# Attention followed by routed experts on one Trainium2 core: raw weight pieces loaded two ahead, gate product two units behind its rows' copy, decoding steps spread anew

## The chip, the cores and the metric

The kernel runs on one core of a Trainium2 chip. The metric is the device time of one execution in microseconds (us); the figure for the kernel before is the median of three runs. Engines: PE is TensorE (matmuls and transposes), DVE is VectorE, ACT is ScalarE, POOL is GpSimd, and SP issues most of the DMAs. Each engine works its own queue of instructions in order.

## What is computed

Three stages, each fed by the one before:

```python
# attention: 4 batches, 8 heads, 768 positions, 64 wide; a local band of 96 and 8 global keys
scores = scale * (q @ k.T) - slope[h] * dist;  a = softmax(where(keep, scores, -1e9));  x = a @ v
# experts: 3072 tokens, each expert takes at most 384, greedily by the highest logit
logits = x @ w_gate
for e in range(8): out[mask_e] = relu(x[mask_e] @ w1[e]) @ w2[e]
# gated network, weights w1, w2, w3, w_out held in float64
y = ((out @ w1) * (out @ w2)) @ w3 @ w_out
```

## The kernel before

**Attention.** The work is 96 items: for each of 16 pairs (a batch b and two heads) three steps p, each with two query tiles, and per step the two heads. A loop over units i (line 383) interleaves them: at every even i it multiplies queries and keys for both heads of a step (`scores`, L313) and reduces them on DVE (L318, bias, scaling and row minimum in one instruction), with the exponential on ACT (L329). Three units later `flip` transposes the probabilities on PE (L342; copied out by ACT, L349), and two more units later `values` multiplies them with v (L362). At a head's last step DVE divides (L368 to L370) into a tile x. A pair is thus six units long.

**Rows and gate.** When both heads of a pair are divided, `rows` (lines 410 to 420) is put into a list `after` for a later unit, twice per pair for three tiles each (z = 0 and 1). It stores x to DRAM, transposes it on PE into a PSUM tile px (L419), and ACT copies that to xt (L420). `gate` (lines 422 to 432) multiplies xt with the gate weights on PE into the last quarter of the same px tile (L427), and DVE adds the result to the logits L (L432; L430 for the first pair of a batch). The pool of px has one buffer: the next `rows` may write it only once L432 has read it. `self.line` keeps PE's attention work in the order in which it is written.

**Decoding.** The last network's weights lie in DRAM as float64 and are decoded to float32 beside attention, 40 pieces of 128x512. `stream` does it in steps: a load into a raw tile (L805, on SP), ACT takes the absolute value of the high words (`size`, L813), POOL clamps it (L837), and DVE puts the bits together (L843, L844, L846). Then ACT and POOL split a piece in two (L202, L207), or a DMA from POOL writes it to DRAM (L851). The function `beside` draws steps from this generator, or from the router's bids while there are any, at slots of each unit: z = 1 before `flip`, z = 2 behind `values`; the table SLOTS says how many. In the program a piece has three steps. Pools: `stage` two raw buffers, `vs` two, `ms` one.

**After attention.** The router searches the first expert's tokens (DVE and PE in turn) while PE folds w3 and w_out together (`fold`); then eight experts run, each with its weights loaded and split, and with the gated network behind it. The plain copies of w1 and w2 are loaded through the same `stream` and `stage` (L802).

**Order.** A scheduler places the instructions on the queues; the lists above fix PE's attention order, and marks keep decoding from moving ahead of attention on DVE and ACT.

Of the kernel before, what the change touches and what calls it, by code (L numbers as in the profile page):

```python
# [147 lines left out]
LAG3 = 2  # L148
# [3 lines left out]
class Net:  # L152
# [84 lines left out]
    def attention(self, ctx, beside, done):  # L237
# [11 lines left out]
        xs = self.pool(ctx, "xs", 2)  # L249
# [3 lines left out]
        ps_x = self.pool(ctx, "ps_x", 1, True)  # L253
# [28 lines left out]
        work = [(b, 2 * g + z, p) for b, g in pairs for p in range(half) for z in range(2)]  # L282
        qk, vs, pr_, pt_, po_, xs_ = {}, {}, {}, {}, {}, {}
# [47 lines left out]
        def flip(b, h, p):  # L331
            pr = pr_.pop((b, h, p))
            todo = [(i, c) for i in range(2) for c in range(len(plan.chunks[2 * p + i]))]
            size = lambda z: plan.chunks[2 * p + z[0]][z[1]][1]
            at = pt_[b, h, p] = {}
            for o in range(0, len(todo), 4):
                grp = todo[o:o + 4]
                pt = ps_t.tile([P, 512], F32, name="one").rearrange("p (c n) -> p c n", n=P)
                ptb = wk.tile([P, 4, P], F32, name=f"ptb{o}")
                for z, (i, c) in enumerate(grp):  # L340
                    c0, m = plan.chunks[2 * p + i][c]
                    self.line(nc.tensor.transpose(pt[:m, z], pr[:, i, c0:c0 + m], self.ident))  # L342
                    at[i, c] = ptb[:m, z]
                z = 0
                while z < len(grp):
                    m, y = size(grp[z]), z + 1
                    while y < len(grp) and size(grp[y]) == m:
                        y += 1
                    nc.scalar.activation(ptb[:m, z:y], pt[:m, z:y], AF.Copy)  # L349
                    z = y  # L350
# [21 lines left out]
        def ahead(f, u):  # L372
            if u < len(pairs):
                f(*pairs[u])

        lag1, lag2 = LAGS
        after = {}
# [2 lines left out]
            for t in range(min(T, 2)):  # L380
                head_bias(t, 0, 0, 1)
        ahead(load, 1)
        for i in range(len(work) + lag2 + 8):
            if i < len(work):
                if i % T == 0:
                    ahead(load_v, i // T)
                    ahead(load, i // T + 2)
                beside(i, 0)
                if i % 2 == 0:
                    scores(work[i][0], work[i][1] // 2, work[i][2])  # L390
            beside(i, 1)
            if 0 <= i - lag1 < len(work):
                flip(*work[i - lag1])
            if 0 <= i - lag2 < len(work):
                w = work[i - lag2]
                values(*w)
                if w[1] % 2 and w[2] == half - 1:
                    b, g = w[0], w[1] // 2
                    x = xs_.pop((b, g))
                    for z in range(2):  # L400
                        after.setdefault(i + LAG3 + 2 * z, []).append((self.rows, (b, g, 3 * z, x, xs, ps_x)))
                        after.setdefault(i + LAG3 + 2 * z + 1, []).append((self.gate, (b, g, 3 * z)))
                    if g == G - 1:
                        after[i + LAG3 + 3].append((done, (b,)))
            beside(i, 2)
            for f, args in after.pop(i, []):
                f(*args)
# [366 lines left out]
class Experts:  # L774
# [41 lines left out]
    def stream(self, todo):  # L816

        nc, V = self.nc, self.nc.vector
        dve = lambda ins: self.net.aside(ins, "dve")
        raw = self.load(*todo[0][:2])
        yield
        m = self.size(raw, todo[0][1])
        yield
        for i, (_, n, v, parts, dst) in enumerate(todo):
            after = self.load(*todo[i + 1][:2]) if i + 1 < len(todo) else None  # L830
            if m is None:
                if v is None:
                    v = raw
                else:
                    nc.scalar.activation(v, raw, AF.Copy)
            else:
                nc.gpsimd.tensor_scalar(m, m, MOST, LEAST, op0=OP.min, op1=OP.max)  # L837
                yield
                if v is None:
                    v = self.vs.tile([P, 512], F32, name="v")[:, :n]  # L840
                pair = raw.bitcast(I32).rearrange("p (n t) -> p n t", t=2)
                lo, hi, mi, vi = pair[:, :, 0], pair[:, :, 1], m.bitcast(I32), v.bitcast(I32)
                dve(V.tensor_scalar(vi, mi, 3, 0x3FFFFFFF, op0=OP.logical_shift_left, op1=OP.bitwise_and))  # L843
                dve(V.scalar_tensor_tensor(vi, hi, -0x40000000, vi, op0=OP.bitwise_and, op1=OP.bitwise_or))  # L844
                yield
                dve(V.scalar_tensor_tensor(vi, lo, 29, vi, op0=OP.logical_shift_right, op1=OP.bitwise_or))  # L846
            if parts is not None:
                parts = parts() if callable(parts) else parts
                self.net.split(*parts, v, nc.scalar, self.low())
            if dst is not None:  # L850
                nc.gpsimd.dma_start(dst, v)  # L851
            if after is not None:
                m, raw = self.size(after, todo[i + 1][1]), after
            yield

    def decode(self):
# [183 lines left out]
PRIME = 28  # L1040
GAP = 1
SOON = 1
SLOTS = (0, 1, 1), (0, 1, 0), (0, 1, 1)
PIN = 3
BEGIN = 7
START = 98
# [6 lines left out]
def steps(gen, n):  # L1053
    for _ in range(n):
        if next(gen, STOP) is STOP:
            return
# [5 lines left out]
def network(ctx, tc, plan, a, out):  # L1062
    net = Net(ctx, tc, plan, a, out)
    ex = Experts(net)
# [1 line left out]
    ex.res2 = net.pool(ctx, "res2", ex.JT // 2)  # L1066
    keep = net.pool(ctx, "keep0")
    ex.ring = net.pool(ctx, "ring", RING)
    ex.stage = net.pool(ctx, "stage", 2)
    ex.vs = net.pool(ctx, "vs", 2)  # L1070
    ex.ms = net.pool(ctx, "ms")
    one = net.pool(ctx, "pone", 1, True)
    net.one = one
    bank = lambda: one.tile([P, 512], F32, name="one")
# [2 lines left out]
    ro = Router(net, ctx)  # L1077
    ro.ps = one
    with ExitStack() as inner:
        decode = ex.decode()  # L1080
        folds = (s for i in range(SOON) for s in ex.fold(i, keep, ex.ring, bank))
        bids = []

        def beside(i, z):
            if i == SETUP and z == 1:
                ro.setup()
            if i >= BEGIN:
                for _ in range(SLOTS[i % 3][z]):
                    if bids and next(bids[0], STOP) is STOP:
                        bids.pop(0)  # L1090
                    elif not bids:
                        steps(decode, 1)
            if i >= START and z == 1:
                steps(folds, RATE)

        net.attention(inner, beside, lambda b: bids.append(ro.bids(slice(b * net.T, (b + 1) * net.T), True)))
        for g in (decode, folds, *bids[:-1]):
            for _ in g:
                pass
        steps(bids[-1], 3)  # L1100
# [15 lines left out]
    inner = ex.rest = ex.inner()  # L1116
# [15 lines left out]
    for i in range(net.E):  # L1132
# [4 lines left out]
        done, soon = False, HEAD  # L1137
        for s, _ in enumerate(ex.run(now, route is None)):
# [8 lines left out]
            elif not done:  # L1147
                if s >= PRIME:
                    done = next(prime, STOP) is STOP
# [29 lines left out]
```

## Time and profile before

| what | before |
|---|---|
| median of 3 runs (range) | 1060.22 us (1055.45 to 1064.94) |
| the profiled execution: time / span | 1060.28 / 1058.5 us |
| PE busy | 1018.3 us (96%) |
| DVE, ACT, POOL busy | 652.7, 397.4, 125.8 us |
| mean granted TensorE clock | 0.963 |
| attention, about 5 to 257 us | PE busy, clock 0.86 |
| experts, 325 us on | PE busy, clock 1.00 |

Times are from one profiled execution; a busy time counts an engine's instructions from start to modelled end. [...] A wait is idle time of an engine just before an instruction, with what ended it.

### The profile page before, as it was taken

The numbers are of one execution on the slowest core, as the hardware profiler recorded it, in microseconds if no ns is written. First come the engines' busy times: TensorE is split into PE (matmuls) and PEld (weight loads), VectorE is DVE, ScalarE is ACT, GpSimd is POOL, SyncE is SP. The second block draws the span as 40 slices with busy tenths as digits, with TensorE's granted clock in tenths as the row PEclk, the third lists the DMA queues.
The fourth block names the chain that finished last, engine by engine and source line by source line (L and its number), as shares of the span: only waits on it lengthen the run. The fifth ranks groups of instructions, "written<-read, shape, count | busy, mean of one in ns | idle before, by whom it ended". The sixth has DMA issues, their size and how long they took to land.

```text
span 1058.5 us, 17537 instructions
## 1 busy us (share of the span) xinstructions
PE 1018.3 (96%) x6348; PEld 931.8 (88%) x6348; DVE 652.7 (62%) x2136; ACT 397.4 (38%) x841; POOL 125.8 (12%) x171
## 2 busy tenths in 40 slices
PE   7999998999989999999999999999999999999996
PEld 6888887888768889999998899999889999999995
DVE  5678676584789773856767485586747556423311
ACT  4677666575225422322422332242133224313311
POOL 1331111223350002001100200110020012001001
PEclk9799788698999999999999999999999999999999
DMA  5677767673015312203200320320132033302100
GB/s 219 193 223 242 246 182 253 217 235 129 16 50 169 110 60 70 91 1 108 91 22 30 112 79 1 110 100 11 41 110 70 2 110 115 105 1 75 35 1 30
DMA packets 53862, 107.57 MB, mean 102 GB/s; under 512 B 5648, under 2 KB 17936, under 8 KB 53776
## 3 DMA queue, kind: packets, MB, share of 16 engines
q1 hardware_dynamic: 48512, 89.65, 26.5%
q0 software_dynamic: 5120, 16.78, 4.6%
q8 instruction: 50, 0.82, 0.3%
q14 instruction: 36, 0.29, 0.1%
q10 hardware_dynamic: 144, 0.02, 0.0%
HBM read 89.65 MB, written 16.78 MB: 101 GB/s over the span
## 4 chain that ended last, share of the span: by engine, by line
PE 72%; issue 9%; DVE 8%; DMA 6%; ACT 4%; POOL 1%; POOLq 0%; SPq 0%; ACTq 0%; DVEq 0%
PE wk L789 11%; PE wk L790 10%; PE wk L791 10%; PE one L789 8%; PE one L791 8%; PE one L790 8%; PE po L362 5%; DMA raw<-in_m_dram 4%; PE one L313 3%; PE one L342 3%; PE one L530 2%; PE px L427 2%; DMA raw<-m_plain 2%; ACT p L329 1%; DVE A L446 1%
## 5 line engine op out<-in xcount | busy, mean ns | idle before, releaser
L789 PE MATMUL wk<-y,res 128*128 128x384 f32 x512 | 176.8, 346 | 0.1
L791 PE MATMUL wk<-y,res 128*128 128x384 f32 x512 | 172.8, 338 | 0.0
L790 PE MATMUL wk<-y,res 128*128 128x384 f32 x512 | 172.4, 337 | 0.1
L1013 DVE TENSOR_TENSOR g<-g,wk 128x384 f32<-128x384 f32 x64 | 35.4, 554 | 129.9 <-PE wk L791 125.2
L202 ACT ACTIVATE w<-wraw 128x512 fp32r<-128x512 f32 x128 | 80.0, 629 | 80.1 <-DMA wraw<-in_w_dram 39.1
L362 PE MATMUL po<-v,ptb 116*128 116x65 f32 (+1 forms) x704 | 105.9, 299 | 2.2 <-PE one L342 2.1
L362 PEld LDWEIGHTS po<-v,ptb 116*128 116x128 f32 (+1 forms) x704 | 103.7, 224 | 4.1 <-PE one L342 3.7
L329 ACT ACTIVATE p<-s,mx 128x232 f32<-128x232 f32 (+1 forms) x192 | 81.9, 466 | 53.6 <-DVE mx L318 53.3
L207 DVE TENSOR_TENSOR w<-wraw,w 128x512 fp32r<-128x512 f32 x128 | 86.2, 687 | 19.5 <-ACT w L202 18.3
L790 PEld LDWEIGHTS wk<-y,res 128*128 128x128 f32 x512 | 96.2, 188 | 2.1 <-DVE y L997 0.4
L789 PEld LDWEIGHTS wk<-y,res 128*128 128x128 f32 x512 | 96.1, 188 | 2.0 <-ACT y L996 0.3
L791 PEld LDWEIGHTS wk<-y,res 128*128 128x128 f32 x512 | 96.1, 188 | 0.0
L1012 ACT ACTIVATE g<-wk 128x384 f32<-128x384 f32 x64 | 31.4, 491 | 152.2 <-PE wk L791 130.1
L789 PE MATMUL wk<-x,w 128*128 128x384 f32 x256 | 87.9, 343 | 0.0
L789 PE MATMUL one<-h,w 128*128 128x384 f32 x256 | 87.0, 340 | 0.0
L791 PE MATMUL one<-h,w 128*128 128x384 f32 x256 | 86.8, 339 | 0.0
L790 PE MATMUL wk<-x,w 128*128 128x384 f32 x256 | 86.6, 338 | 0.1
L790 PE MATMUL one<-h,w 128*128 128x384 f32 x256 | 86.3, 337 | 0.0
L791 PE MATMUL wk<-x,w 128*128 128x384 f32 x256 | 86.1, 336 | 0.0
L318 DVE CUSTOM_DVE_ANT_0 s<-one,bias 128x232 f32<-128x232 f32 (+1 forms) x192 | 66.3, 374 | 30.5 <-PE one L313 30.2
L922 POOL DMA_INDIRECT xg<-x_rows,idx x24 | 25.4, 1057 | 482.8 <-issue 398.5
L1015 ACT ACTIVATE h<-g 128x384 fp32r<-128x384 f32 x64 | 33.4, 522 | 120.7 <-DVE g L1013 120.7
(186 smaller groups left out, 2033.5 us busy)
## 6 DMA issues: line engine op xcount, KB each, us to landing
wraw<-in_w_dram SPq DMA_DIRECT2D x128, 256.0 KB, 2.8
raw<-in_m_dram SPq DMA_DIRECT2D x32, 512.0 KB, 4.6
v<-in_v_dram SPq DMA_DIRECT2D x32, 357.5 KB, 3.4
k<-in_k_dram SPq DMA_DIRECT2D x16, 404.0 KB, 6.0
q<-in_q_dram SPq DMA_DIRECT2D x16, 384.0 KB, 3.9
x_rows<-x SPq DMA_DIRECT2D x32, 192.0 KB, 5.4
raw<-in_mo_dram SPq DMA_DIRECT2D x8, 512.0 KB, 4.8
m_plain<-v POOLq DMA_DIRECT2D x16, 256.0 KB, 4.6
```

Source lines behind the costliest of these rows:

```text
L202: self.aside(he.activation(hi, raw, AF.Copy), "act")
L207: self.aside(le.tensor_tensor(lo[:, c], raw[:, c], hi[:, c].bitcast(F32), op=OP.subtract), "dve" if le is self.nc.vector else "pool")
L313: self.line(nc.tensor.matmul(banks[y][:, 256 * z:256 * z + m], q[r, qt], k[r, kt], start=True, stop=True))
L318: self.mark["dve"] = nc.vector.tensor_tensor_reduce(out=s[y][:, i, c0:c0 + m], in0=banks[y][:, 256 * z:256 * z + m], in1=head_bias(2 * p + ...
L329: self.mark["act"] = nc.scalar.activation(pr[:, i, :n], s[y][:, i, :n], AF.Exp, bias=m1, scale=-1.0)
L342: self.line(nc.tensor.transpose(pt[:m, z], pr[:, i, c0:c0 + m], self.ident))
L362: self.line(nc.tensor.matmul(po[:, t], at[i, c], v[:m, plan.nch[t] + c], start=c == 0, stop=c == last))
L789: mm(out, w[0], x[0], start=start, stop=False)
L790: mm(out, w[0], x[1], start=False, stop=False)
L791: self.net.beat = mm(out, w[1], x[0], start=False, stop=stop)
L1013: V.tensor_tensor(g, g, two[1], op=OP.mult)
L1015: nc.scalar.activation(h[:, 0], g, AF.Copy)
```

## The change

In `stream` two raw pieces are under way ahead of the one being decoded, instead of one, and `stage` has three buffers. In `attention` the second `rows` of a pair comes three units behind the first instead of two, and each `gate` two units behind its `rows` instead of one; the loop is a unit longer. SLOTS is now a table over six units instead of three: as many steps per six units (ten), with one step behind `values` in the units where a head is divided (i mod 6 is 3 and 4) and none before `flip`. The pools `vs` and `ms` move into the attention's own scope. In the changed file lines behind 825 stand one further down (L843, L844, L846 are L844, L845, L847).

```diff
@@ -380,7 +380,7 @@
             for t in range(min(T, 2)):
                 head_bias(t, 0, 0, 1)
         ahead(load, 1)
-        for i in range(len(work) + lag2 + 8):
+        for i in range(len(work) + lag2 + 9):
             if i < len(work):
                 if i % T == 0:
                     ahead(load_v, i // T)
@@ -398,10 +398,10 @@
                     b, g = w[0], w[1] // 2
                     x = xs_.pop((b, g))
                     for z in range(2):
-                        after.setdefault(i + LAG3 + 2 * z, []).append((self.rows, (b, g, 3 * z, x, xs, ps_x)))
-                        after.setdefault(i + LAG3 + 2 * z + 1, []).append((self.gate, (b, g, 3 * z)))
+                        after.setdefault(i + LAG3 + 3 * z, []).append((self.rows, (b, g, 3 * z, x, xs, ps_x)))
+                        after.setdefault(i + LAG3 + 3 * z + 2, []).append((self.gate, (b, g, 3 * z)))
                     if g == G - 1:
-                        after[i + LAG3 + 3].append((done, (b,)))
+                        after[i + LAG3 + 5].append((done, (b,)))
             beside(i, 2)
             for f, args in after.pop(i, []):
                 f(*args)
@@ -822,12 +822,13 @@
 
         nc, V = self.nc, self.nc.vector
         dve = lambda ins: self.net.aside(ins, "dve")
-        raw = self.load(*todo[0][:2])
+        raws = [self.load(*z[:2]) for z in todo[:2]]
         yield
-        m = self.size(raw, todo[0][1])
+        m = self.size(raws[0], todo[0][1])
         yield
         for i, (_, n, v, parts, dst) in enumerate(todo):
-            after = self.load(*todo[i + 1][:2]) if i + 1 < len(todo) else None
+            raw = raws.pop(0)
+            raws += [self.load(*z[:2]) for z in todo[i + 2:i + 3]]
             if m is None:
                 if v is None:
                     v = raw
@@ -849,8 +850,8 @@
                 self.net.split(*parts, v, nc.scalar, self.low())
             if dst is not None:
                 nc.gpsimd.dma_start(dst, v)
-            if after is not None:
-                m, raw = self.size(after, todo[i + 1][1]), after
+            if raws:
+                m = self.size(raws[0], todo[i + 1][1])
             yield
 
     def decode(self):
@@ -1040,7 +1041,7 @@
 PRIME = 28
 GAP = 1
 SOON = 1
-SLOTS = (0, 1, 1), (0, 1, 0), (0, 1, 1)
+SLOTS = ((0, 1, 1),) * 3 + ((0, 0, 1),) * 2 + ((0, 1, 1),)
 PIN = 3
 BEGIN = 7
 START = 98
@@ -1066,9 +1067,7 @@
     ex.res2 = net.pool(ctx, "res2", ex.JT // 2)
     keep = net.pool(ctx, "keep0")
     ex.ring = net.pool(ctx, "ring", RING)
-    ex.stage = net.pool(ctx, "stage", 2)
-    ex.vs = net.pool(ctx, "vs", 2)
-    ex.ms = net.pool(ctx, "ms")
+    ex.stage = net.pool(ctx, "stage", 3)
     one = net.pool(ctx, "pone", 1, True)
     net.one = one
     bank = lambda: one.tile([P, 512], F32, name="one")
@@ -1077,6 +1076,8 @@
     ro = Router(net, ctx)
     ro.ps = one
     with ExitStack() as inner:
+        ex.vs = net.pool(inner, "vs", 2)
+        ex.ms = net.pool(inner, "ms")
         decode = ex.decode()
         folds = (s for i in range(SOON) for s in ex.fold(i, keep, ex.ring, bank))
         bids = []
@@ -1085,7 +1086,7 @@
             if i == SETUP and z == 1:
                 ro.setup()
             if i >= BEGIN:
-                for _ in range(SLOTS[i % 3][z]):
+                for _ in range(SLOTS[i % 6][z]):
                     if bids and next(bids[0], STOP) is STOP:
                         bids.pop(0)
                     elif not bids:
```

PE, a pair in the middle of attention, before: px<-ident,x is `rows`, px<-wg,xt is `gate`, one<-k,q the scores, one<-ident,p `flip`, po<-v,ptb `values`.

```order
L419 MATMUL px<-ident,x 128x128 x3
L342 MATMUL one<-ident,p 116x128 x4
L362 MATMUL po<-v,ptb_1329 128x65 x4
L427 MATMUL px<-wg,xt 128x8 x3
L313 MATMUL one<-k,q 128x232 x4
L342 MATMUL one<-ident,p 116x128 x4
L362 MATMUL po<-v,ptb_1389 128x65 x4
L419 MATMUL px<-ident,x 128x128 x3
L342 MATMUL one<-ident,p 128x128
L342 MATMUL one<-ident,p 116x128 x2
L362 MATMUL po<-v,ptb_1425 128x65 x4
L427 MATMUL px<-wg,xt 128x8 x3
```

The same place now.

```order
L419 MATMUL px<-ident,x 128x128 x3
L342 MATMUL one<-ident,p 116x128 x4
L362 MATMUL po<-v,ptb_1323 128x65 x4
L313 MATMUL one<-k,q 128x232 x4
L342 MATMUL one<-ident,p 116x128 x4
L362 MATMUL po<-v,ptb_1376 128x65 x4
L427 MATMUL px<-wg,xt 128x8 x3
L342 MATMUL one<-ident,p 128x128
L342 MATMUL one<-ident,p 116x128 x2
L362 MATMUL po<-v,ptb_1408 128x65 x4
L419 MATMUL px<-ident,x 128x128 x3
L313 MATMUL one<-k,q 128x232 x4
```

Between a `rows` and its `gate` there stood one flip and one values; now a scores, a second flip and a second values stand there too. Between the first gate and the second `rows` there stood scores, flip and values; now flip and values.

DVE at the first gate of a later pair, before: `s,mx<-one,bias` are the four score reductions of a step (each with a read of its minimum, mx), res<- and v<- is decoding, L<-L,px reads px.

```order
L318 ISA s,mx_1574<-one,bias_160 128x232
L318 ISA mx_1574 128x1
L318 ISA s,mx_1575<-one,bias_140 128x128
L318 ISA mx_1575 128x1
L318 ISA s,mx_1576<-one,bias_160 128x232
L318 ISA mx_1576 128x1
L843 TENSOR_SCALAR res<-m 128x512
L432 TENSOR_TENSOR L<-L,px 128x24
L844 SCALAR_TENSOR_TENSOR res<-raw,res 128x512
L846 SCALAR_TENSOR_TENSOR res<-raw,res 128x512
```

The same place now; ahead of these rows stands the first of the four reductions, and each is followed by its read.

```order
L847 SCALAR_TENSOR_TENSOR res<-raw,res 128x512
L318 ISA s,mx_1637<-one,bias_160 128x232
L318 ISA mx_1637 128x1
L844 TENSOR_SCALAR res<-m 128x512
L318 ISA s,mx_1638<-one,bias_160 128x232
L318 ISA mx_1638 128x1
L845 SCALAR_TENSOR_TENSOR res<-raw,res 128x512
L318 ISA s,mx_1639<-one,bias_160 128x232
L318 ISA mx_1639 128x1
L847 SCALAR_TENSOR_TENSOR res<-raw,res 128x512
L432 TENSOR_TENSOR L<-L,px 128x24
L368 TENSOR_SCALAR r<-po 128x6
```

The read of px has moved behind the reductions of one more step, with four decoding instructions among them.

SP near its start, before: raw<-in_mo_dram are raw weight pieces.

```order
L805 DMA raw<-in_mo_dram 128x1024 x2
L287 DMA q<-in_q_dram 128x768
L289 DMA k<-in_k_dram 128x808
L295 DMA v<-in_v_dram 128x715
L287 DMA q<-in_q_dram 128x768
L295 DMA v<-in_v_dram 128x715
L805 DMA raw<-in_mo_dram 128x1024
L289 DMA k<-in_k_dram 128x808
L805 DMA raw<-in_mo_dram 128x1024
```

The same place now.

```order
L805 DMA raw<-in_mo_dram 128x1024 x3
L287 DMA q<-in_q_dram 128x768
L289 DMA k<-in_k_dram 128x808
L295 DMA v<-in_v_dram 128x715
L805 DMA raw<-in_mo_dram 128x1024
L295 DMA v<-in_v_dram 128x715
L287 DMA q<-in_q_dram 128x768
L289 DMA k<-in_k_dram 128x808
L805 DMA raw<-in_mo_dram 128x1024
```

Three raw loads instead of two go out at the start; further on the loads keep the same mixture with q, k and v, one piece earlier.

## Rows read from the trace of the kernel before

**Rows 1.** Windows: us; busy (count) of PE, PEld, DVE, ACT, POOL; clock; DMA.

```profile
5.00:257.00 252.00, 238.50 (x1663) 211.23 (x1664) 172.74 (x750) 163.52 (x397) 49.69 (x74) 0.86 0.69 220
...
325.00:1058.00 733.00, 718.57 (x4325) 672.74 (x4325) 426.17 (x1181) 211.95 (x406) 44.54 (x45) 1.00 0.20 66
```

**Rows 2.** Waits of PE from 5 to 250 us: total, times, longest.

```profile
PE px L427 <- ACT xt L420: 8.5, 10, 2.7
...
PE po L362 <- PE one L342: 2.1, 5, 0.7
PE one L313 <- DVE mx L318: 2.0, 5, 0.7
```

**Rows 3.** Timeline of PE: start, us, instruction, idle before it.

```profile
38.27 0.83 PE L427 MATMUL px<-wg,xt 128*128 128x8 f32 x6 [1.21 <-ACT xt L420]
...
117.67 0.83 PE L427 MATMUL px<-wg,xt 128*128 128x8 f32 x6 [1.17 <-ACT xt L420]
...
151.93 0.84 PE L427 MATMUL px<-wg,xt 128*128 128x8 f32 x6 [0.80 <-ACT xt L420]
...
184.86 1.45 PE L427 MATMUL px<-wg,xt 128*128 128x8 f32 x6 [2.67 <-ACT xt L420]
...
247.52 0.83 PE L427 MATMUL px<-wg,xt 128*128 128x8 f32 x6 [1.54 <-ACT xt L420]
```

**Rows 4.** Windows inside the five stretches of attention at clock 0.50.

```profile
41.00:57.00 16.00, 16.00 (x78) 14.62 (x78) 10.38 (x36) 10.30 (x26) 6.67 (x9) 0.50 0.68 207
...
249.00:255.00 6.00, 6.00 (x32) 5.43 (x29) 2.28 (x11) 3.17 (x8) 1.13 (x2) 0.50 0.39 123
sum 68.00, PE 66.89 PEld 59.42 DVE 37.30 ACT 35.55 POOL 14.41; mean PE 13.38 PEld 11.88 DVE 7.46 ACT 7.11 POOL 2.88
```

**Rows 5.** Window, the longest stretch of attention at full clock.

```profile
58.00:117.00 59.00, 56.69 (x478) 50.58 (x477) 47.78 (x208) 45.32 (x109) 12.44 (x18) 1.00 0.77 239
```

**Rows 6.** Timeline of ACT ahead of the wait at 184.86 us.

```profile
182.65 0.66 ACT L813 ACTIVATE m<-raw 128x512 f32<-128x512 f32 x1 [1.39 <-DMA raw<-in_m_dram]
...
184.34 0.47 ACT L420 ACTIVATE xt<-px 128x384 f32<-128x384 f32 x1
```

**Rows 7.** Waits of ACT for raw pieces, 10 to 245 us.

```profile
ACT m L813 <- DMA raw<-in_m_dram: 9.3, 12, 1.4
```

**Rows 8.** Timeline of PE at full clock, two units of a pair.

```profile
111.81 0.79 PE L427 MATMUL px<-wg,xt 128*128 128x8 f32 x6
112.53 1.05 PE L313 MATMUL one<-k,q 64*128 64x232 f32 x8
...
114.84 0.50 PE L419 MATMUL px<-ident,x 128*128 128x128 f32 x3
115.17 0.49 PE L342 MATMUL one<-ident,p 128*128 128x128 f32 x3
```

**Rows 9.** Timeline of PE and DVE: scores, their reductions with decoding between.

```profile
147.15 1.05 PE L313 MATMUL one<-k,q 64*128 64x232 f32 x8
...
148.24 0.40 DVE L318 CUSTOM_DVE_ANT_0 s<-one,bias 128x232 f32<-128x232 f32 x1 [0.73 <-PE one L313]
...
150.24 0.43 DVE L843 TENSOR_SCALAR res<-m 128x512 int32<-128x512 int32 x1 [1.27 <-POOL m L837]
150.58 0.39 DVE L318 CUSTOM_DVE_ANT_0 s<-one,bias 128x232 f32<-128x232 f32 x1
...
150.90 0.69 DVE L844 SCALAR_TENSOR_TENSOR res<-raw,res 128x512 int32<-128x512 int32 x1
...
152.88 0.18 DVE L432 TENSOR_TENSOR L<-L,px 128x24 f32<-128x24 f32 x1 [0.30 <-PE px L427]
```

**Rows 10.** Waits of DVE's decoding for POOL, 10 to 245 us.

```profile
DVE v L843 <- POOL m L837: 5.6, 5, 2.2
DVE res L843 <- POOL m L837: 4.8, 7, 1.3
```

**Rows 11.** Waits from 255 to 420 us.

```profile
ACT res L202 <- DMA raw<-m_plain: 14.6, 10, 4.3
```

## The prediction

> **What bounds the kernel now.** The windows by stage come first. From 325 us on PE is busy 718.57 of 733 us at clock 1.00 [rows 1]: the experts are bound by PE, and nothing in the change touches their products. What can move is attention, 252 us in which PE also counts as busy (238.50 us) but at a mean clock of 0.86 [rows 1]. [...]
>
> Next, PE's waits in attention. They are few: 8.5 us in all at L427 (`gate`) for ACT's copy xt, then 2.1 and 2.0 us at two others, of which none is longer than 0.7 us [rows 2]. The timeline shows where the long ones lie: 1.21, 1.17, 0.80, 2.67 and 1.54 us, all at L427, and each 1 or 2 us ahead of one of the five stretches, or, at 184.86, on its edge [rows 3]. Five waits of 0.80 us or more, five falls; no wait up to 0.7 us [rows 2] stands alone ahead of a fall. So I read `gate` as what costs attention its clock. Why xt is late shows on ACT's timeline ahead of the worst one: L813 waits 1.39 us for a raw piece, three exponentials stand behind it, and only then comes L420 [rows 6]. ACT waited so 12 times, 9.3 us, at most 1.4 us [rows 7]. At 117.67 there is no late raw piece: there ACT merely had exponentials and copies queued ahead of xt. Both parts of the change aim at this place.
>
> **What the five stretches cost.** Inside them five windows hold 68 us [rows 4] and 78, 81, 45, 89 and 32 matmuls, 325 in all (the first and last are shown). At full clock PE did 478 in 59 us [rows 5], 8.10 per us. The 325 would have taken 325/8.10 = 40.1 us, so the stretches cost 68 - 40.1 = 27.9 us, 5.6 each. [...]
>
> **Gate two units behind its rows.** At full clock the time between two units' starts can be read off: a unit with scores takes 112.53 to 114.84 = 2.31 us, a `gate` 111.81 to 112.53 = 0.72 us [rows 8], and a unit without scores from 115.17 [rows 8] to where the gate at 117.67 began its wait of 1.17 us [rows 3], 116.50: 1.33 us. Before, xt had one unit of 1.33 us to be made in; now it has that and one with scores, 1.33 + 2.31 = 3.64 us. The longest lateness, 2.67 us [rows 3], is 0.36 us over the 2.31 us gained; the other four are well under it. I take all 8.5 us of [rows 2] as gone, and with them the cause of all five falls: -8.5 and -27.9 us.
>
> **Raw pieces two ahead.** A load now goes out three steps earlier, and ten steps lie in six units, so about 1.8 units, some 3 us of full-speed time; the longest wait was 1.4 us [rows 7]. ACT's 9.3 us go. They are not added again: PE felt them only through xt. The third buffer frees no transfer that SP must wait longer for: load i+2 needs the buffer of piece i-1, as load i+1 did of two. What is queued behind a waiting raw load on SP (q, k, v and x stores) is what it was. DMA was busy 0.69 of 252 us [rows 1], 174 us; in attention 36 us shorter that is a share of 0.81, and in a full-speed stretch it was 0.77 [rows 5] without PE waiting for k, q or v. I take nothing; if a transfer came late, a wait like those of [rows 7] would be back on ACT, whose cover is now 2.31 us longer.
>
> **Fewer steps at the divisions.** The number of steps in six units is the same, so DVE does the same work; x comes earlier, but no wait of PE for x stands in [rows 2], so it is worth nothing by itself. DVE was busy 47.78 of 59 us at full clock and ACT 45.32 [rows 5]: neither takes over as the bound. The steps go into the unit ahead, and there they matter, as follows.
>
> **The wait that the change adds.** px has one buffer, so the second `rows` (L419) must wait for L432, which reads the first gate's product. Before, 2.31 us of PE's work stood between; now one flip and one values, 1.33 us, and L432 stands in DVE's order behind the four reductions of the step's scores and the decoding among them. Reckoned from the start of those scores on PE: L419 is reached at 2.31 + 0.72 + 1.33 = 4.36 us. DVE's first reduction starts 148.24 - 147.15 = 1.09 us after the scores; a reduction takes a pitch of 0.32, a shift (now L844) a pitch of 0.34, the two longer decoding instructions 0.69, L432 0.18 [rows 9]. In the pair shown in the new order, four reductions, one shift and three long ones: 1.09 + 1.28 + 0.34 + 2.07 + 0.18 = 4.96 us, so PE waits 0.6 us. Over the 16 pairs the new order has this mixture three times, two shifts and two long ones twice (4.61, a wait of 0.25), and lighter ones eleven times (4.27 at most, no wait). Sum 3 x 0.6 + 2 x 0.25 = 2.3 us. From below the cost is nothing, since DVE may find PE later than I reckon. From above: a shift ahead of L432 may wait for POOL, which happened 12 times for 10.4 us, 0.87 us each and at most 2.2 [rows 10]; 16 x 0.87 = 14 us, and falls of the clock besides. I take 2.5 us, near the worked pattern. The next pair's `rows` has 2.31 us behind the second gate, and L432 there has only two division instructions and one of decoding ahead: no wait.
>
> **The ends.** The loop's extra unit holds no product; the last gate comes later by a fold product or two. I take 1 us (0 to 2). Behind attention the plain copies are loaded further ahead too; ACT waited 14.6 us for them [rows 11], but PE was busy 98% of the time from 325 us on [rows 1], so ACT's wait was covered: nothing.
>
> **Sum.** -8.5 - 27.9 + 2.5 + 1 = -32.9 us if no fall is left. I don't believe in none. The waits that remain reach 0.7 us [rows 2], the new one is 0.6, and 0.80 was enough [rows 3]. One stretch that stays or comes anew costs 5.6 + 0.8 = 6.4 us. With one: -26.5. The profiled execution took 1060.28 us (span 1058.5), as the median, 1060.22: 1060.3 - 26.5 = 1034.
>
> **The rivals.**
> A, forecast: none to two stretches are left. None 1027, one 1034, two 1040; with no new wait and no fall 1023. For it: every long wait was at one place, and that place gets 2.31 us. Chance 0.66.
>
> B: the wait moves from L427 to L419, where the single px buffer now sits between DVE and PE, and three to six falls remain: 1047, 1053, 1059, 1066. For it: a reckoned 0.6 us, and POOL's 0.87 us [rows 10] on top would pass 0.80. Against it: five pairs of 16 are heavy, and DVE waited for PE at L432 (0.30 us at 152.88 [rows 9]) rather than the other way. [...] Chance 0.21.
>
> C, slower: L432 is late by 0.80 us or more in most pairs, because the shift ahead of it waits for POOL nearly every time. A fall and a wait cost 6.4 us; the break-even is 32.9/6.4 = five falls, and with eight it is 1060.3 - 32.9 + 51 = 1078. Chance 0.08.
>
> D: the change doesn't do what it says: xt is late by more than the new room, because ACT itself is behind by units, and the falls come from PE's thin work rather than from waits. Then 1055 to 1060. Against it: 59 us ran at full clock with the same work [rows 5]. Chance 0.05.
>
> **Range and chances.** A reaches from 1023 to about 1041; adding B's first cases up to 1053 takes in 0.8. A change of 1% (10.6 us) is about what a measurement of this kernel can tell from none. Faster by more: A, and B with three falls, 0.75. Within 1%: the rest of B to six falls, and D: 0.17. Slower: C, 0.08.
>
> **What would show it.** Right, if PE's wait for xt at L427 is under 1 us in all, ACT's wait for raw pieces near nothing, clock over 0.95 in attention, and attention about 26 us shorter with the experts' span unchanged. The new wait would stand as L419 behind L432, at 2 to 3 us. Wrong, if PE waits at L419 for 0.80 us or more and half-speed stretches follow it (B, C); if half-speed stretches begin where PE did not wait (D), which would undo my reading of their cause; or if the stretches are gone and attention is still long, by waits for DVE or a transfer.

## The result

The changed kernel takes 1027.41 us (median of 4 runs, 1026.38 to 1032.16), the kernel before beside it 1057.84 (4 runs, 1054.03 to 1064.94): a ratio of 0.9714, interval 0.9650 to 0.9777. That is 2.9% faster and 6.6 us below the forecast of 1034, inside its range. The profiled execution took 1026.38 us, span 1024.6 against 1058.5. Ratios, here and below, are of mean times without the runs over 1.5% above the fastest of their kernel, so they can stand a little nearer to 1 than the medians do.

Windows by stage of the kernel after (us; busy time and count of PE, PEld, DVE, ACT, POOL; the mean clock that the profile shows as granted to TensorE, as a share with 1.00 the highest in these traces; DMA share; GB/s): attention, the folds between, the experts. Under them the page's row of the granted clock in 40 slices.

```profile
5.00:225.00 220.00, 210.24 (x1673) 186.85 (x1674) 175.05 (x750) 164.56 (x399) 54.77 (x76) 0.94 0.79 254
225.00:291.00 66.00, 57.95 (x352) 45.02 (x350) 50.11 (x171) 20.24 (x36) 26.32 (x32) 1.00 0.13 39
291.00:1024.00 733.00, 718.00 (x4325) 672.79 (x4325) 425.92 (x1181) 211.59 (x406) 44.81 (x45) 1.00 0.21 66
PEclk9989997999999999999999999999999999999999
```

The experts are what they were, 733 us with PE busy 718.00 [rows 1]. The last `gate` runs at 238 us where it ran at 272: nearly all of the 33.9 us came from attention, whose mean clock rose from 0.86 [rows 1] to 0.94.

PE's waits from 5 to 250 us (total, times, longest), all of attention's of 0.5 us in total and more; two of the router, 1.0 and 0.9 us at L530, come behind the last `gate`:

```profile
PE px L419 <- DVE L L432: 8.5, 7, 2.5
PE one L313 <- DMA k<-in_k_dram: 5.4, 1, 5.4
PE one L313 <- DVE mx L318: 0.7, 1, 0.7
```

The wait for the load of k is at the start of the program (5.4 us) and was there before (5.3 us). The wait for xt at L427 [rows 2] is gone entirely. In its place stands one of exactly the same sum at L419, for which 2.5 us had been forecast. PE's timeline shows its five longest:

```profile
48.94 0.55 PE L419 MATMUL px<-ident,x 128*128 128x128 f32 x3 [1.79 <-DVE L L432]
...
103.95 0.55 PE L419 MATMUL px<-ident,x 128*128 128x128 f32 x3 [0.80 <-DVE L L432]
...
156.36 0.90 PE L419 MATMUL px<-ident,x 128*128 128x128 f32 x3 [2.54 <-DVE L L432]
...
189.46 0.55 PE L419 MATMUL px<-ident,x 128*128 128x128 f32 x3 [1.64 <-DVE L L432]
...
216.59 0.55 PE L419 MATMUL px<-ident,x 128*128 128x128 f32 x3 [0.80 <-DVE L L432]
```

Three half-speed stretches (clock 0.50) are left where five were [rows 4]; in windows of one microsecond each those five reach from about 40.5 to 57.5, 119 to 136, 153 to 163.5, 184 to 204.5 and 249 to 255.5 us, and between them the clock is 1.00. The three begin at the ends of the three waits of 1.64 us or more, from 0.3 us before to 1.3 us behind, by such windows. These lie inside them:

```profile
51.00:60.00 9.00, 9.00 (x46) 8.40 (x45) 5.99 (x26) 5.65 (x14) 2.57 (x4) 0.50 0.86 270
157.00:169.00 12.00, 12.00 (x59) 10.55 (x58) 6.87 (x27) 5.60 (x15) 1.89 (x4) 0.50 0.86 266
191.00:193.00 2.00, 2.00 (x11) 1.43 (x8) 1.68 (x8) 0.78 (x3) 0.77 (x2) 0.50 0.77 143
```

With their edges, as one-microsecond windows give them, they hold 10.2 + 13.6 + 3.4 = 27.2 us; those of before hold 71.7 us counted the same way.

Why L432 was late shows on DVE, whose instructions from 151.02 to 156.22 us stand in the trace in the program's order. Before two of the three, its order held a decoding shift that waited for the last write of a decoded piece to leave buffer v:

```profile
153.95 0.43 DVE L844 TENSOR_SCALAR v<-m 128x512 int32<-128x512 int32 x1 [1.92 <-DMA m_plain<-v]
...
156.13 0.17 DVE L432 TENSOR_TENSOR L<-L,px 128x24 f32<-128x24 f32 x1
...
188.89 0.43 DVE L844 TENSOR_SCALAR v<-m 128x512 int32<-128x512 int32 x1 [2.51 <-DMA m_plain<-v]
...
189.23 0.17 DVE L432 TENSOR_TENSOR L<-L,px 128x24 f32<-128x24 f32 x1
```

Ahead of the one at 48.94 there was no such wait, only the reductions with a shift and two long decoding instructions among them in front of L432, of which one took 1.12 us where [rows 9] have 0.69. The waits on the decoding chain from 10 to 245 us (after): ACT hardly waits for raw pieces (9.3 us before [rows 7]), DVE hardly for POOL (10.4 us [rows 10]), but DVE now waits 5.0 us for v (1.3 before):

```profile
DVE v L844 <- DMA m_plain<-v: 5.0, 3, 2.5
...
ACT m L813 <- DMA raw<-in_m_dram: 2.1, 4, 1.3
DVE v L844 <- POOL m L838: 1.0, 3, 0.5
DVE res L844 <- POOL m L838: 0.9, 3, 0.5
```

### The profile page after: what moved, and what is told of

It is laid out like the page before. It is cut to its first block, busy times and chain, and to the rows that moved or that the text cites. A ratio compares the mean times of both kernels' runs of the same rounds, so it can differ in the third digit from the quotient of the medians.

```text
span 1024.6 us, 17539 instructions
## 1 busy us (share of the span) xinstructions
PE 986.2 (96%) x6348; PEld 904.7 (88%) x6348; DVE 655.2 (64%) x2136; ACT 397.7 (39%) x841; POOL 128.8 (13%) x171
## 3 DMA queue, kind: packets, MB, share of 16 engines
q1 hardware_dynamic: 48512, 89.65, 27.9%
## 4 chain that ended last, share of the span: by engine, by line
PE 75%; issue 10%; DVE 10%; DMA 3%; ACT 1%; POOL 1%; POOLq 0%; DVEq 0%; SPq 0%; ACTq 0%
PE wk L789 11%; PE wk L790 11%; PE wk L791 11%; PE one L789 8%; PE one L791 8%; PE one L790 8%; PE po L362 5%; PE one L313 4%; PE one L342 4%; PE one L530 3%; PE px L427 2%; DMA raw<-m_plain 1%; PE px L419 1%; DMA m_plain<-v 1%; DVE s L318 1%
## 5 line engine op out<-in xcount | busy, mean ns | idle before, releaser
L362 PE MATMUL po<-v,ptb 116*128 116x65 f32 (+1 forms) x704 | 94.2, 277 | 0.0
L362 PEld LDWEIGHTS po<-v,ptb 116*128 116x128 f32 (+1 forms) x704 | 91.8, 202 | 0.4 <-issue 0.2
L329 ACT ACTIVATE p<-s,mx 128x232 f32<-128x232 f32 (+1 forms) x192 | 78.7, 466 | 29.8 <-DVE mx L318 29.3
L923 POOL DMA_INDIRECT xg<-x_rows,idx x24 | 24.8, 1033 | 481.4 <-issue 321.5
L789 PE MATMUL one<-W,h 128*128 128x512 f32 x192 | 76.3, 397 | 0.0
```

What stands on the lines that cost most here:

```text
L329: self.mark["act"] = nc.scalar.activation(pr[:, i, :n], s[y][:, i, :n], AF.Exp, bias=m1, scale=-1.0)
L362: self.line(nc.tensor.matmul(po[:, t], at[i, c], v[:m, plan.nch[t] + c], start=c == 0, stop=c == last))
L789: mm(out, w[0], x[0], start=start, stop=False)
```

## The experiments

The change has three parts: the gate's move, the raw pieces two ahead, the new table. Three kernels put one part into the kernel before, three take one part out of the kernel after; four more go at the wait at L419, one joins what helped, and one makes xt late. "Gate" in the table means the whole move, of the second `rows` too, and "raw" takes in the third `stage` buffer and the pools' move; these were not separated further. p_gate, p_raw, p_slots and m_gate were timed on one chip and the other experiments on another, each beside runs of the kernel before. Half-speed time is worked out for each run as 2 x (1 - mean granted clock) x span, the median over the runs; some 5 us of it lie at the end of the program, outside attention (4.3 us in before, 5.0 in after, by windows of one microsecond). Where a fence shows waits they are from attention, one profiled execution each.

| kernel | gate | raw | table | median us (runs) | range | half-speed us | ratio, interval |
|---|---|---|---|---|---|---|---|
| before | | | | 1052.6 to 1058.0 | 1038 to 1082 | 81 | 1 |
| p_gate | new | | | 1044.07 (10) | 1033 to 1058 | 52 | 0.9940, 0.9872 to 1.0008 |
| p_raw | | new | | 1052.93 (10) | 1041 to 1064 | 83 | 0.9998, 0.9934 to 1.0062 |
| p_slots | | | new | 1058.86 (10) | 1050 to 1072 | 76 | 1.0032, 0.9972 to 1.0092 |
| m_gate | | new | new | 1060.94 (4) | 1057 to 1063 | 93 | 1.0105, 0.9988 to 1.0222 |
| m_raw | new | | new | 1039.76 (10) | 1032 to 1053 | 46 | 0.9882, 0.9831 to 0.9933 |
| m_slots | new | new | | 1021.51 (4) | 1019 to 1026 | 18 | 0.9711, 0.9613 to 0.9810 |
| after | new | new | new | 1027.41 (4) | 1026 to 1032 | 31 | 0.9714, 0.9650 to 0.9777 |

### One part alone, and one part undone

The gate's move (undone in m_gate):

```diff
-                        after.setdefault(i + LAG3 + 2 * z, []).append((self.rows, (b, g, 3 * z, x, xs, ps_x)))
-                        after.setdefault(i + LAG3 + 2 * z + 1, []).append((self.gate, (b, g, 3 * z)))
+                        after.setdefault(i + LAG3 + 3 * z, []).append((self.rows, (b, g, 3 * z, x, xs, ps_x)))
+                        after.setdefault(i + LAG3 + 3 * z + 2, []).append((self.gate, (b, g, 3 * z)))
...
```

The raw pieces two ahead, with `stage` of three buffers and the pools moved (undone in m_raw):

```diff
-        raw = self.load(*todo[0][:2])
+        raws = [self.load(*z[:2]) for z in todo[:2]]
...
-            after = self.load(*todo[i + 1][:2]) if i + 1 < len(todo) else None
+            raw = raws.pop(0)
+            raws += [self.load(*z[:2]) for z in todo[i + 2:i + 3]]
...
```

The table (undone in m_slots):

```diff
-SLOTS = (0, 1, 1), (0, 1, 0), (0, 1, 1)
+SLOTS = ((0, 1, 1),) * 3 + ((0, 0, 1),) * 2 + ((0, 1, 1),)
...
```

Expected of p_gate: 

> Only the gate is moved two units behind its rows; raw pieces one ahead and the steps' table as before. Theory G (the gate's wait for xt is the root of the half-speed stretches): no wait at L427 over 0.3 us, the stretches that began there are gone, new waits of L419 behind L432 of 5 to 10 us with two or three stretches; 1030 to 1040 us. Rival R (raw pieces that come late on ACT are the root): exponentials and copies still come late, waits move to other places, 1050 to 1058. Rival S (DVE is late where heads are divided, and that sets the pace): 1045 to 1058, and the pace at full clock stays near 8.1 matmuls per us.

Expected of p_raw: 

> Only the raw pieces are loaded two ahead in three buffers (with the pools' move). Theory G: at least three of the five waits at L427 stay, since at 117.67 us xt was late without a late raw piece; 1045 to 1058. Rival R: ACT's waits for raw pieces fall below 2 us, L427 waits under 0.5 us each, 1027 to 1037. Rival S: 1050 to 1058.

Expected of p_slots: 

> Only the steps' table is changed. Theory G and rival R: the waits at L427 and for raw pieces stay, 1050 to 1060. Rival S: the pace at full clock goes from 8.1 towards 8.7 matmuls per us and the time to 1035 to 1045, with the stretches at L427 still there.

Expected of m_gate: 

> The changed kernel without the gate's move: raw pieces two ahead and the new table, gate one unit behind as before. Theory G: long waits at L427 are back, 1042 to 1055. Rivals R and S together: 1027 to 1033, as the changed kernel, or less, since the wait of L419 behind L432 (8.5 us) is gone as well.

Expected of m_slots: 

> The changed kernel with the old table of steps: gate two units behind, raw pieces two ahead. Theory GR (gate and raw pieces together do it, since each alone left the other's lateness: 1044 and 1053 us): 1025 to 1035, pace at full clock as in the changed kernel. Rival S (the table carries the pace): 1035 to 1045, with waits of scores or copies on DVE and ACT of 2 us or more.

Expected of m_raw: 

> The changed kernel with raw pieces one ahead in two buffers: gate two units behind, new table. Theory GR: ACT waits for raw pieces again (8 to 11 us), 1038 to 1048, like the gate alone. Rival S: 1025 to 1033, since gate and table are enough.

Measured: no part alone comes near the whole. Of the medians, the gate alone gives some 13 us and the raw pieces alone some 4 (the intervals of both take in no difference), the table nothing. The two that matter, together and without the table, give 36, and the interval of m_slots overlaps neither that of p_gate nor that of p_raw. Without the gate's move nothing at all is left of the gain (m_gate); taken out of the kernel after, the raw pieces cost 12 us (m_raw). So the theories that the raw pieces or the table carry the change fell, and so did the plain one that the gate's move carries it: it is the two together.

The waits say how they join. Without the gate's move PE still waits for xt, with the raw pieces alone (first row, p_raw; this profiled execution was its longest, 1064.5 us) and with the table besides (second row, m_gate):

```profile
PE px L427 <- ACT xt L420: 7.4, 8, 1.7
...
PE px L427 <- ACT xt L420: 13.2, 17, 1.3
```

With the gate's move alone that wait is gone, but ACT still waits for raw pieces, DVE for POOL behind it, and PE waits at other places (p_gate):

```profile
ACT m L813 <- DMA raw<-in_m_dram: 12.1, 10, 2.2
...
DVE res L843 <- POOL m L837: 7.7, 6, 2.7
...
DVE v L843 <- POOL m L837: 6.2, 7, 2.5
...
PE one L313 <- DVE mx L318: 3.6, 7, 0.9
...
PE po L362 <- PE one L342: 3.0, 6, 0.7
```

Two of its five half-speed stretches, at 78 and 133 us, stand at the end of such a chain. A late raw piece makes DVE's shift wait for POOL; behind the shift DVE comes late to the division, L370, or to L432, and PE to the buffer that these free:

```profile
76.16 0.68 ACT L813 ACTIVATE m<-raw 128x512 f32<-128x512 f32 x1 [1.91 <-DMA raw<-in_m_dram]
...
77.56 0.43 DVE L843 TENSOR_SCALAR res<-m 128x512 int32<-128x512 int32 x1 [1.92 <-POOL m L837]
...
78.12 0.56 DVE L370 TENSOR_TENSOR x<-po,r 128x384 f32<-128x384 f32 x1
...
78.79 1.51 PE L362 MATMUL po<-v,ptb 128*128 128x65 f32 x6 [1.70 <-issue]
...
127.60 0.66 ACT L813 ACTIVATE m<-raw 128x512 f32<-128x512 f32 x1 [2.17 <-DMA raw<-in_m_dram]
...
128.99 0.43 DVE L843 TENSOR_SCALAR res<-m 128x512 int32<-128x512 int32 x1 [2.68 <-POOL m L837]
...
133.43 0.90 PE L419 MATMUL px<-ident,x 128*128 128x128 f32 x3 [1.15 <-DVE L L432]
```

(For the wait put to "issue" see the last section.) Two more stretches, at 58 and 181 us, begin behind waits of 0.87 and 0.85 us for the reductions of the scores, with DVE busy on decoding ahead of them; how much of these the raw pieces made is not shown.

In m_raw ACT waited 19.8 us for raw pieces and DVE 11.1 us for POOL at v alone. With both parts and the old table (m_slots) three of PE's waits are left over 1 us in total:

```profile
PE po L362 <- PE one L342: 2.5, 6, 0.7
PE px L419 <- DVE L L432: 1.3, 2, 0.9
PE po L362 <- issue: 1.2, 1, 1.2
```

PE's waits in attention, that for k left out, sum to 12.6 us in before, 11.0 in p_gate, 9.2 in after and 5.9 in m_slots. DVE's waits for v come with the raw pieces (6.5 us in p_raw, 5.4 in m_slots, 0.8 in m_raw), but in m_slots L419 has only 1.3 us. So L419's 8.5 us in the kernel after came with the table: it puts up to four decoding instructions of a pair ahead of L432. In exchange PE's waits at L362, 3.7 us in m_slots (the first and last of these rows), are gone in the kernel after. That the table costs time as well is likely (medians 1021.5 and 1027.4) but not settled: the two weren't timed side by side, and their ratios to before are 0.9711 and 0.9714.

### The wait at L419

x_px2 gives the second `rows` a PSUM buffer of its own, from the pool that the scores use, in all but the last pairs:

```diff
-                        after.setdefault(i + LAG3 + 3 * z, []).append((self.rows, (b, g, 3 * z, x, xs, ps_x)))
+                        after.setdefault(i + LAG3 + 3 * z, []).append((self.rows, (b, g, 3 * z, x, xs, self.one if z and i < 86 else ps_x)))
...
```

x_vs3 gives v a third buffer, so that DVE needn't wait for the write; x_both has the two together; b_vs3 is m_slots with v's third buffer:

```diff
-        ex.vs = net.pool(inner, "vs", 2)
+        ex.vs = net.pool(inner, "vs", 3)
```

Expected of x_px2: 

> The changed kernel with a second PSUM buffer for the second rows of all but the last two pairs (the bank that the folds use later). Theory W (the 8.5 us of L419 behind L432 and the stretches behind three of these waits are what is left to gain): L419 waits under 1 us, stretches at 50, 156 and 190 us gone, 27 us of half speed worth 11 to 13 us, in all 1005 to 1012. Rival V (DVE is late there because its decoding waits for the buffers of plain copies, and the lateness shows at the next place): 1016 to 1027, with waits at scores or values instead.

Expected of x_vs3: 

> The changed kernel with three buffers instead of two for decoded pieces on their way to DRAM, one PSUM buffer px as it is. Theory V (DVE stands ahead of L432 in a wait for these buffers; two of the three stretches of the changed kernel follow such a wait): DVE's wait for them under 1 us, L419 waits for L432 halved to about 4 us, 1018 to 1023. Rival W (the order of DVE's work ahead of L432 alone makes it late): 1025 to 1031.

Expected of x_both: 

> As the one before, and three buffers instead of two for decoded pieces on their way to DRAM. Theory W: the waits of decoding for these buffers (5.0 us) go, but PE does not feel them any more, same as with the second PSUM buffer alone within 4 us. Rival V: 5 to 12 us faster than with the second PSUM buffer alone.

Expected of b_vs3: 

> Gate two units behind and raw pieces two ahead with the old table of steps (1021.5 us), and three buffers for decoded pieces. Theory V: its 5.4 us of waits for these buffers go; half-speed time was 18 us there, so 4 to 8 us are to be had: 1013 to 1018. Rival: the waits were covered, 1019 to 1024.

| kernel | median us (4 runs each) | range | half-speed us | L419 behind L432, us | ratio, interval |
|---|---|---|---|---|---|
| x_px2 | 1029.11 | 1024 to 1031 | 34 | 1.1 | 0.9763, 0.9663 to 0.9863 |
| x_vs3 | 1024.04 | 1020 to 1034 | 27 | 6.7 | 0.9774, 0.9713 to 0.9835 |
| x_both | 1017.16 | 1013 to 1022 | 24 | 1.1 | 0.9654, 0.9559 to 0.9749 |
| b_vs3 | 1016.90 | 1013 to 1022 | 16 | 0.4 | 0.9706, 0.9637 to 0.9775 |

x_px2 took 7.4 of the 8.5 us of waiting at L419 away (the line is L420 there, L433 the product's reader) and the time didn't move. That the wait at px is what costs the kernel after its last falls did not hold: DVE still stood 4.6 us at v, and PE met the lateness elsewhere. In the profiled execution three stretches stayed, 34 us of them. The longest stands behind a wait that the profile puts to "issue"; this wait ended 0.1 us behind DVE's division, which had come late by DVE's wait for v:

```profile
177.78 0.43 DVE L845 TENSOR_SCALAR v<-m 128x512 int32<-128x512 int32 x1 [2.67 <-DMA m_plain<-v]
...
178.34 0.56 DVE L370 TENSOR_TENSOR x<-po,r 128x384 f32<-128x384 f32 x1
...
179.00 1.51 PE L362 MATMUL po<-v,ptb 128*128 128x65 f32 x6 [2.45 <-issue]
```

The third buffer alone took DVE's waits for v out of the trace, but L419 kept 6.7 us; the four decoding instructions still stood ahead of L432. Only the two together, or v's third buffer with the old table, gave some 10 us more than the kernel after by the medians, which were not timed side by side; x_both and x_px2 were, and no run of x_both (1013 to 1022) was as long as the shortest of x_px2 (1024 to 1031).

### Everything that helped, in one kernel

b_all is m_slots with both: v in three buffers, and a second px buffer (`i < 92`).

Expected of b_all: 

> As the one before, and a second PSUM buffer for the second rows of all pairs but the last. If L419's wait for L432 (1.3 us in two waits with the old table) still costs a stretch: 1008 to 1013, mean granted clock 0.995 or more. Rival: nothing is left there with the old table, the same as the one before within 4 us.

Measured: 1014.56 us (4 runs: 1012.96, 1013.01, 1016.11, 1027.06), ratio 0.9735, interval 0.9633 to 0.9838, against runs of before with a median of 1052.58. By its median it is the shortest of all here, 12.8 us under the kernel after, but the two weren't timed side by side and the intervals overlap; from b_vs3, timed beside it, it can't be told. The run of 1027.06 us had 43 us at half speed, the other three 4 to 6. Its profiled execution has no half-speed stretch in attention; its window and the page's row of the clock:

```profile
5.00:218.00 213.00, 208.56 (x1720) 185.05 (x1720) 175.75 (x754) 165.05 (x404) 56.69 (x80) 1.00 0.79 262
PEclk9999999999999999999999999999999999999998
```

### xt made late

c_late is m_slots with xt sent through 5, 7 or 9 copies on POOL ahead of the first gate of six pairs; each copy multiplies by 1, and no work is left out.

```diff
+        late = {(0, 3): 5, (1, 1): 7, (1, 3): 9, (2, 1): 5, (2, 3): 7, (3, 1): 9}.get((b, g), 0) if h == 0 else 0
...
+            for _ in range(late - 1):
+                nc.gpsimd.tensor_scalar(flat(t2), flat(t2), 1.0, None, op0=OP.mult)
...
```

Expected: 

> Gate two units behind and raw pieces two ahead with the old table (1021.5 us, about 18 us at half speed), and in six pairs, at the first gate, xt is passed through 5, 7 or 9 extra copies on POOL (0.5 to 0.7 us each), so that PE waits there: nothing or little at 5, 1 to 3 us at 7 and 9. The results are the same, it only costs time. Theory G (a wait of about 1 us makes the clock fall): a half-speed stretch begins within 3 us behind each wait of 1 us or more, four stretches of some 10 to 17 us more than in the base, 40 to 60 us at half speed, 1042 to 1055. Rival D (the clock falls on PE's thin work, whenever): the stretches lie elsewhere, half-speed time stays near 18 us, and the time grows by the waits alone, 5 to 10 us.

Measured: 1088.35 us (6 runs, 1084.65 to 1095.35), ratio 1.0381, interval 1.0322 to 1.0441; 105 us at half speed against 18 in m_slots. The waits came out longer than meant. Five of the six, and windows at four:

```profile
78.08 0.99 PE L435 MATMUL px<-wg,t 128*128 128x8 f32 x6 [3.38 <-POOL t L427]
...
113.67 1.45 PE L435 MATMUL px<-wg,t 128*128 128x8 f32 x6 [6.96 <-POOL t L427]
...
161.56 1.45 PE L435 MATMUL px<-wg,t 128*128 128x8 f32 x6 [9.24 <-POOL t L427]
...
236.90 1.45 PE L435 MATMUL px<-wg,t 128*128 128x8 f32 x6 [4.24 <-POOL t L427]
...
279.92 1.45 PE L435 MATMUL px<-wg,t 128*128 128x8 f32 x6 [10.21 <-POOL t L427]
```

```profile
80.00:84.00 4.00, 4.00 (x19) 3.00 (x19) 1.42 (x4) 0.95 (x3) 0.59 (x1) 0.50 0.36 105
108.00:142.00 34.00, 28.33 (x132) 25.33 (x134) 13.40 (x50) 12.35 (x31) 7.75 (x9) 0.52 0.36 111
157.00:177.00 20.00, 15.44 (x74) 13.85 (x75) 8.11 (x37) 5.58 (x15) 6.89 (x8) 0.50 0.41 124
236.00:250.00 14.00, 13.10 (x63) 11.76 (x63) 5.35 (x20) 4.25 (x11) 2.68 (x4) 0.50 0.34 109
```

(The one left out, at 198.04, waited 3.55 us.) The six waits sum to 37.6 us, the time rose by 67 us over m_slots: here a late xt costs more than its wait, and at all six, of 3 us and more, half speed stood behind. Some 17 us of the half-speed time lie inside the waits themselves, where no matmul ran; the other 70 us of the rise from 18 to 105, at 0.42 us each (next section), make 29 us by this estimate, and 37.6 + 29 is near the 67 found. So rival D fell, and theory G had the order but not the size. Of waits of about 1 us, the range of the kernel before [rows 3], this run has one at 221.51, 0.74 us at L313, with a stretch from 222 to 233 us behind it, and one at 31.65, 0.73 us at L362, with none.

### What a microsecond at half speed costs

Over 45 runs of the kernel before, timed beside these experiments, time is close to 1025 + 0.42 x half-speed time (r = 0.92; one run of 2415 us and one whose clock is out of line left out; with the second kept in, the slope is 0.31 and r 0.76). So the spread of that kernel, 1038 to 1082 us, goes mostly with the length of its half-speed stretches. Taking 0.42 times the half-speed time off each run, as if that slope held for every kernel, leaves as medians 1022 to 1023 for p_gate and m_raw, which have the gate's move without the raw pieces, and 1014 for m_slots and after, which have both: by this estimate the raw pieces are worth 7 to 9 us there besides what the clock gives. Alone they leave 1020 (p_raw), where before leaves 1024.

## Why the prediction came out near

**The half-speed stretches as the cost: right, and sized well.** The rows gave 27.9 us for 68 us, 0.41 per us. The slope over runs is 0.42.

**Gate two units behind: right at L427, not enough for the clock.** All 8.5 us of [rows 2] went, as worked out. That all five falls would go with them was wrong in the part alone: p_gate has no wait at L427 and 52 us at half speed.

**Raw pieces two ahead, priced at nothing: the step that failed.** It rested on "PE felt them only through xt". In p_gate a late raw piece also reaches PE through POOL and DVE, at the division and at L432, with half speed behind both. On top of the gate's move the part is worth 22.6 us (p_gate to m_slots, medians from two chips), without it nothing that the interval shows. The sum held because the forecast put these us on the gate's move, whose falls it counted as gone; as the change has both parts, the fault doesn't show in the total, and that is luck.

**The new wait at L419: right place, mis-sized, 2.5 us forecast and 8.5 found,** inside the bounds of 0 to 14 but with three falls behind it. The reckoned 0.6 us per heavy pair left out DVE's wait for v at L844, 1.92 and 2.51 us ahead of two of the three, and at the third a decoding instruction took 1.12 us where 0.69 had been reckoned; the bound from above had looked at POOL (which fell to 1.9 us) as what the shift waits for. In the kernel after three falls stand behind waits for px, of 1.79, 2.54 and 1.64 us; but x_px2, in which 1.1 of the 8.5 us at px are left, kept three falls, so px alone is not the cause. One of the three stands behind a wait of 2.45 us for another PSUM buffer, po, which a late DVE held.

**Falls left: one forecast, three found.** By its count of falls the result is rival B's picture, at a time near the 1027 that A gives for none. The prediction's own sign of being wrong came about: L419 waited 0.80 us or more, with half speed behind three of these waits. Of its signs of being right, L427 and ACT's raw pieces held, attention came out 32 us shorter where about 26 was said, and its clock 0.94 where over 0.95 was. Half-speed time fell from 71.7 to 27.2 us; 44.5 x 0.41 = 18 us, where 27.9 - 5.6 = 22.3 had been taken.

**What was not in the sum: the pace at full clock.** The longest such stretch of after:

```profile
62.00:121.00 59.00, 57.61 (x506) 51.81 (x504) 51.67 (x225) 46.41 (x115) 9.59 (x13) 1.00 0.81 259
```

That is 506/59 = 8.58 matmuls per us against 8.10 [rows 5]; over the some 193 us of attention at full clock that makes about 11 us, an estimate. Other long stretches of the kernels with the raw pieces two ahead ran at 8.41 to 8.53, of those without at 7.91 to 8.39, at different places, and some records can be missing. Over most of attention's full-clock time, from 20 us on, it is 7.8 in before, 7.9 in p_raw, 8.1 in p_gate and m_raw, 8.2 in m_slots and 8.4 in after, so the pace rose, but which part raised it is not shown. Account: -18 (clock) - 11 (pace) - 8.5 (L427) + 8.5 (L419) = -29 of the 33.9 us; the rest isn't assigned. So 1027 for 1034 is a near total over three terms that were off and partly cancelled: L419 by +6, the falls left by +4, the pace by -11.

**That 0.80 us is enough for a fall and up to 0.7 us makes none: wrong as a rule.** In after, waits of 0.80 us at 103.95 and 216.59 have no fall behind them. In p_gate a stretch begins at 215 us behind waits of 0.25 and 0.15 only.

**The table, worth nothing by itself: held,** and it put the steps ahead of L432 as said. **Ends and plain copies: held.** The experts' span is unchanged, and ACT's wait for the plain copies, covered before [rows 11], fell from 14.6 to 8.2 us without moving anything.

## What to carry to other kernels

Where a stage runs at a mean clock below full, price the half-speed stretches by their matmuls at the full-clock pace of the same stage; here that gave 0.41 us per us at half speed, and the slope over 45 runs is 0.42. Here a late transfer reached the bottleneck by more than one queue (in p_gate 1.91 us of ACT's waiting for a raw piece, 1.92 of DVE's for POOL, then 1.70 of PE's), so look for the next path before pricing at nothing the part that makes it early; two parts can be worth much more together than the sum of each alone, here 36 us against 13 and 4 by the medians. When a wait moves to a single buffer, list everything in the other engine's order ahead of the releasing instruction, its own waits for buffers that a write must free included.

## What the runs showed that was not expected

In these runs a wait of a given length does not decide by itself whether the clock falls. The same instruction, waiting 0.72 and 0.73 us at the same place, had about 24 us at half speed behind it in b_vs3 and none in b_all. (Nor had it in p_gate, p_raw, m_slots and c_late, where it waited 0.72 to 0.74 us.) PE's timeline and the window behind, first of b_vs3, then of b_all:

```profile
29.65 1.37 PE L362 MATMUL po<-v,ptb 128*128 128x65 f32 x6 [0.72 <-PE one L342]
...
30.00:52.00 22.00, 22.00 (x105) 19.63 (x105) 11.72 (x43) 11.34 (x27) 7.40 (x10) 0.50 0.58 185
```

```profile
31.97 0.85 PE L362 MATMUL po<-v,ptb 128*128 128x65 f32 x6 [0.73 <-PE one L342]
...
32.00:54.00 22.00, 22.00 (x195) 20.03 (x195) 21.60 (x74) 20.02 (x49) 14.94 (x18) 1.00 0.89 283
```

One kernel differs as much from run to run: the four runs of b_vs3 had 29, 4, 26 and 6 us at half speed.

Each of p_gate, p_raw, m_slots, m_raw and x_px2 has one wait of PE of 1.1 to 2.5 us at L362 that the profile puts to "issue", and a half-speed stretch behind it. In all five PE starts 0.1 us behind the end of DVE's division L370, which reads po, at the first `values` of the same head in the next pair; po has two buffers, one for each head. So do the shorter waits at L362 that the profile, here and in [rows 2], puts to L342: these five and 40 shorter ones, of 0.17 us and more, in nine traces all end 0.09 to 0.11 us behind a division. So what PE stands for is, as these times have it, the po buffer that a late DVE still reads. Ahead of the division in the five DVE had waited for v (1.29 us in p_raw, 1.44 in m_slots, 2.67 in x_px2) or for POOL (1.92 in p_gate); in m_raw it was busy decoding. In x_vs3, x_both, b_vs3 and b_all, which have v's third buffer, no such wait of over 0.73 us stands.

What, beside the wait, decides whether a wait of about 1 us is followed by a fall stays open: the runs show only that fewer and shorter waits in attention go with less half-speed time, from 81 us in before to 5 us in b_all.
